# Forgetting attention and a SwiGLU block on one core: a planner with new transfer times, loads ahead of transposes, one load for both gate sums, one pool of four PSUM banks

## The chip, the core and the metric

The kernel runs on one core of a Trainium2 chip. The time is the device time of one execution in microseconds; less is better. The profile is taken from one execution of its own, whose time stands beside its span in the table below.

Engine names as in the profile: PE (matmuls; PEld is its weight load), DVE, ACT, POOL, and SP (SyncE, which only issues DMA transfers). Sixteen DMA engines carry all transfers.

## The reference, cut to what matters

Inputs are q, k, v with 8 batches, 8 heads, 576 positions and 64 values per head, and a forget gate f per batch, head and position. Attention is causal, with a decay from the running sum of log f:

```
scores = scale * q @ k.T
cum    = cumsum(log(clip(f, 1e-4, 1)))          # the "gate sum" of a head, 576 numbers
scores = where(causal, -1e9, scores + cum[:, None] - cum[None, :])
attn   = softmax(scores) @ v                     # 64 heads in all
x      = attn.transpose(0, 2, 1, 3).reshape(4608, 512)
out    = (silu(x @ w_gate) * (x @ w_val)) @ w_out    # 512 -> 1536 -> 512
```

The row term `cum[:, None]` drops out of the softmax, so the kernel only adds the column term.

## The kernel before

**Pairs and units.** The 64 heads are handled as 32 pairs (p = 0 to 31, four pairs per batch); the two heads of a pair lie in partitions 0 to 63 and 64 to 127. A pair has two units: g = 0 holds row blocks 0 to 3 of 64 queries, g = 1 row blocks 4 to 8. The first four pairs run all their g = 0 units first, then g = 1; later pairs run g = 1, then g = 0.

**What a pair goes through.** K and Q are loaded as float32 (`load_pair`, L325: 96 and 72 partitions), cast to bf16 on POOL (L350, L352), transposed on PE into a PSUM bank (L364) and copied to `kt` and `qz` (L378, L380). The gate sums of all heads are computed once at the start and stored to DRAM (`cum_f`, L312); for each later pair they are loaded again, each head's row repeated over 64 partitions, into a tile `cb` of 128 partitions by 576 numbers. That is one transfer per head (L332):

```
for h in range(2):
    loads["cb", p, h] = pl.op({"SP": 600}, lambda e, h=h: nc.sync.dma_start(
        out=pl.buf(("cb", p))[64 * h:64 * h + 64, :],
        in_=cum_dram[2 * p + h:2 * p + h + 1, :].to_broadcast((64, S))), ...
```

Scores come from PE (L399, with the causal mask added by L403), DVE adds the gate sum and takes the minimum (L415), ACT takes the exponential with its row sum (L429), POOL multiplies by the reciprocal sum into `pk` (L464). P is then transposed: for pairs 0 to 7 on PE (L488, L493), for pairs 8 to 31 by a DMA transpose on SP's queue (L476), 19 slices of 128 by 128 for g = 1 and 6 for g = 0. PE forms the weighted sum with V (L514), and DVE or ACT copies it into `xT` (L538), a ring of 2560 token columns.

**Feed-forward.** Tokens go through in tiles of 256 or 512: gate and value products (L595), tanh on ACT (L601), two DVE products (L603, L606), projection in rows of 128 tokens (`project`, L620), a copy to `ot` (L630, L632) and a store (L637).

**The order.** Nothing is scheduled at run time. `Plan.order` lists all operations once, when the program is built: each operation has one or more possible engines with a planned duration, a priority, and a planned time from its end to its users; transfers have a planned time on the wire (`dma`). Repeatedly the operation that can start earliest is taken, lower priority number first. Buffers are given out pool by pool in a fixed turn. Each engine then runs its operations strictly in that order and waits where data or a buffer is not there. SP's queue, too, is one fixed sequence of loads, transposes and stores. `after` lists make the planner place an operation later; they are no waits on the chip. `SPARE` makes the planner prefer POOL over ACT or DVE for some operations. Attention has lower priority numbers than feed-forward, so it goes first where both could start.

**PSUM.** Eight banks: `sp` 2 (scores), `tx` 2 (K and Q transposes, weighted sums), `gv` 3 (gate and value products, P transposes on PE, the last projections), `op` 1 (projection).

**Buffers of the loads.** `kf`, `qf` 2 each, `kt`, `qz` and `cb` 5 each, `pk` and `pT` 2 each per unit kind, `vf` 2, `ot` 2.

Of the kernel before, what the change touches and what calls it, by code (L numbers as in the profile page):

```python
# [15 lines left out]
HUGE = 3.0e38  # L16


class Op:
    __slots__ = ("n", "engs", "fn", "reads", "writes", "prio", "lat", "dma", "deps", "start", "end", "eng", "after", "holds", "bias")  # L20

    def __init__(self, n, engs, fn, reads, writes, prio, lat, dma, after, holds):
        self.holds = list(holds)
        self.n, self.engs, self.fn, self.reads, self.writes = n, engs, fn, reads, writes
        self.prio, self.lat, self.dma, self.after = prio, lat, dma, after
        self.start = self.end = self.eng = None
        self.bias = {}


class Plan:  # L30
# [6 lines left out]
    def __init__(self):  # L37
        self.ops, self.pools, self.home, self.where, self.turn = [], {}, {}, {}, {}
# [4 lines left out]
    def key(self, key, pool, turn=None):  # L43
        self.home[key], self.turn[key] = pool, turn
# [9 lines left out]
    def order(self):  # L54
# [14 lines left out]
        turn = {name: [] for name in self.pools}  # L69
# [4 lines left out]
        for k in sorted(self.home, key=rank):  # L74
            turn[self.home[k]].append(k)
        taken = {name: 0 for name in self.pools}
# [3 lines left out]
        free = {e: 0 for e in ("PE", "DVE", "ACT", "POOL", "SP")}  # L80
        wire = {True: 0, False: 0}
        ready = {o.n: 0 for o in self.ops if not waiting[o.n]}
        done = []

        def room(o):

            at, take = 0, []
            for k in o.writes:
                if k not in self.home or k in self.where:
                    continue  # L90
                name, best = self.home[k], None
                if turn[name][taken[name] + sum(name == self.home[x] for x, _ in take)] != k:
# [10 lines left out]
                take.append((k, best[1]))  # L103
            return at, take

        while ready:
            best = None
            for n, r in ready.items():
                o = self.ops[n]
                got = room(o)  # L110
                if got is None:
                    continue
                for e, dur in o.engs.items():
                    s = max(r, got[0], free[e])
                    c = (s + o.bias.get(e, 0), o.prio, n, e, dur, got[1])
                    if best is None or c[:4] < best[:4]:
                        best = c
# [4 lines left out]
            s -= o.bias.get(e, 0)  # L122
            for k, b in take:
                name = self.home[k]
                self.where[k] = b
                slots[name][b] = k
                taken[name] += 1
            o.start, o.eng = s, e
            free[e] = s + dur
            if o.dma:  # L130
                q = e == "POOL"
                at = max(wire[q], free[e] + 600)
# [3 lines left out]
                o.end = wire[q] + 1200  # L136
# [21 lines left out]
def kernel(  # L158
# [41 lines left out]
    AHEAD = 8  # L200
    BEHIND = 5
    BOTH = 8
    LAG = 3.5
    EASE = (2.5, 3)
    SPARE = {"ACT": 300, "DVE": 600}
    EARLY = {0: 4.3, 1: 7.8}
    FREE = 8
    STARTUP = "p0 f9 f0 p1 c1 p2 c2 p3 v00 c3 v01 wg0 wv0 wg2 wv2 v02 v03 v04 wg4 wv4 wg8 wv8 p4 c4 wo0 p5 c5 wo4 wo8 p6 c6 v10 v11 v12"
# [48 lines left out]
    bufs("gv", [P, 512], F32, 3, ps)  # L257
    bufs("op", [P, 512], F32, 1, ps)
# [36 lines left out]
    def gates(key, parts, np_, prio):  # L295
        x = lambda: pl.buf(key)[0:np_, :]
        for n, (a, z, src) in enumerate(parts):
            loads["f", key, n] = pl.op({"SP": 600}, lambda e, a=a, z=z, src=src: nc.sync.dma_start(out=pl.buf(key)[a:z, :], in_=src),
                                       (), [(key, 0)] + [key] * (n == 0), prio + n * .01, dma=500)
# [8 lines left out]
    for p in range(NDIRECT):  # L308
# [4 lines left out]
          [("fa", 3)], ["cum_dram"], -120, dma=500, lat=0, holds=["fa"])  # L313
# [6 lines left out]
    def load_pair(p):  # L320
        b, hp = divmod(p, NPB)
        s = first[p]
        for name, src, pr in (("k", k, 0), ("q", q, .1)):
# [4 lines left out]
                (), [(name + "f", p)], (-99 + 3 * p if p < NPB else s) + pr, dma=1130 if name == "k" else 980, after=[sums[p - 3, 0 if p - 3 >= NPB else 1]] if p >= NPB else [])  # L328
        if p >= NDIRECT:
            pl.key(("cb", p), "cb")  # L330
            for h in range(2):
                loads["cb", p, h] = pl.op({"SP": 600}, lambda e, h=h: nc.sync.dma_start(  # L332
                    out=pl.buf(("cb", p))[64 * h:64 * h + 64, :],
                    in_=cum_dram[2 * p + h:2 * p + h + 1, :].to_broadcast((64, S))),
                    ["cum_dram"], [("cb", p), (("cb", p), 3)], -98.5 + 3 * p if p < NPB else s + .2, dma=560)

    def prepare(p):
        s = first[p]
        for name in ("k", "q"):
# [19 lines left out]
            pl.key(tk, "tx")  # L359
# [5 lines left out]
            pl.op({"PE": KC * (KR / 2.4 + 2.5)}, transpose, [bk], [tk], s - 1, lat=200)  # L365
            halves = [(0, P, None)] if name == "k" else [(0, 64, 0), (64, 128, 1)]
            ok = ("kt", p) if name == "k" else ("qz", p)
            pl.key(ok, ok[0])
            for a, z, h in halves:
# [11 lines left out]
                pl.op({"ACT": 600, "DVE": 680}, evac, [tk] + ([("z", "qz", p)] if h is not None and p < 5 else []), [ok], s - .9)  # L381
# [4 lines left out]
    def scores(p, g):  # L386
# [3 lines left out]
        for n, bank in enumerate(BANKS[g]):  # L390
# [14 lines left out]
            pl.op({"PE": mm(*cols)}, mult, [("kt", p), ("qz", p), "mask"], [sk], pr, lat=220)  # L405
# [29 lines left out]
    def normalize(p, g):  # L435
# [11 lines left out]
        pl.op({"DVE": 95}, lambda e: nc.vector.reciprocal(lr(), lr()), [("lr", p, g)], [("l2", p, g)], s, lat=100, holds=[("lr", p, g)])  # L447
# [27 lines left out]
        if (p, g) not in ON_PE:  # L475
            pl.op({"SP": 550 + 150 * NSL[g]}, lambda e: nc.sync.dma_start_transpose(  # L476
                out=pl.buf(tk), in_=pl.buf(kk).rearrange("p s k -> p (s k)")),
                [kk], [tk], s - 1, dma=186 * NSL[g])
            return
        for a in range(0, NSL[g], 8):  # L480
            z = min(a + 8, NSL[g])
            bk = ("tt", p, g, a)
            pl.key(bk, "gv")
# [5 lines left out]
            pl.op({"PE": 56 * (z - a)}, transpose, [kk], [bk], s, lat=200)  # L489
# [6 lines left out]
    def weighted(p, gs):  # L496
        b, hp = divmod(p, NPB)
        keys, cost = [], 190
        for g in gs:
            pl.key(("xo", p, g), "tx", at[p, gs[0]] + (LAG if p >= NPB else EASE[g]))  # L500
# [15 lines left out]
        pl.op({"PE": cost}, mult, [("pT", p, g) for g in gs] + [("vt", b, c) for c in range(max(HI[g] for g in gs) // 2 + 1)],  # L516
              keys, at[p, gs[0]], lat=220, holds=[("vt", b)])
        for g in gs:
            spread(p, g)

    def spread(p, g):
# [5 lines left out]
        for a, z in ((0, cut), (cut, w)):  # L527
# [12 lines left out]
            o = pl.op({"ACT": QB * (z - a) * .833 + 130, "DVE": QB * (z - a) / .96 + 85}, evac, [xk],  # L540
                      [("x", hp, n) for n in range(tok[0] // QB, tok[1] // QB)], s)
            evacs.append((o, tok))

    def load_v(b):
        for c in range(5):
# [4 lines left out]
            if b:  # L550
                s = at[b * NPB, 1] + c * .1 - .5
# [3 lines left out]
                (), [fk], s, dma=1500 * n / P, after=wait)  # L555
# [7 lines left out]
    def weights():  # L563
# [4 lines left out]
        for a, z in zip(cuts, cuts[1:]):  # L568
            for nm, wt, src in (("wg", wg, moe_w_gate), ("wv", wv, moe_w_val)):
                piece({"POOL": 600}, lambda e, wt=wt, src=src, a=a, z=z: nc.gpsimd.dma_start(  # L570
                    out=wt[:, :, a:z], in_=src[:, a:z].rearrange("(ko p) n -> p ko n", p=P)),
                    (), [(nm, n) for n in range(a // P, z // P)], 2 + a / 256, dma=4.7 * (z - a) + 900)
        for c in range(0, KF, 4):
            piece({"POOL": 600}, lambda e, c=c: nc.gpsimd.dma_start(
                out=wo[:, c:c + 4, :], in_=moe_w_out[c * P:(c + 4) * P, :].rearrange("(ko p) n -> p ko n", p=P)),
                (), [("wo", n) for n in range(c, c + 4)], 7 + c / 4, dma=3300)
# [3 lines left out]
    def gate(t, tok, n):  # L580
# [3 lines left out]
        for u in range(KF // nf):  # L584
# [3 lines left out]
            for nm, wt in (("wg", wg), ("wv", wv)):  # L588
                bk = (nm, t, u)
                pl.key(bk, "gv", EARLY[t] + u * .55 if t in EARLY else None)  # L590
# [18 lines left out]
    def project(t, tok, n):  # L609
        nf = 512 // n  # L610
        for ms in range(n // P):
            bk = ("op", t, ms)
            end = (t, ms) == (len(TILES) - 1, n // P - 1)
            pl.key(bk, "gv" if t >= len(TILES) - 2 and (ms or t == len(TILES) - 1) else "op")
            pr = 1000 + (t + 1) * 20 + (ms + .5) * 12 * P / n
            for f0 in range(0, KF, 4):
                def mult(e, f0=f0, ms=ms, bk=bk):
                    for fc in range(f0, f0 + 4):
                        hh = pl.buf(("hh", t, fc // nf))
                        nc.tensor.matmul(pl.buf(bk), hh[:, (fc % nf) * n + ms * P:(fc % nf) * n + ms * P + P], wo[:, fc, :],  # L620
                                         start=fc == 0, stop=fc == KF - 1)
                pl.op({"PE": mm(*[DM] * 4)}, mult, [("hh", t, fc // nf) for fc in range(f0, f0 + 4)] +
                      [("wo", fc) for fc in range(f0, f0 + 4)] + ([(bk, f0)] if f0 else []), [bk, (bk, f0 + 4)], pr, lat=220)
            ok = ("ot", t, ms)
            pl.key(ok, "ot")

            for a, z in ((0, DM // 2), (DM // 2, DM)) if end else ((0, DM),):
                def evac(e, bk=bk, ok=ok, a=a, z=z):
                    if e == "ACT":
                        nc.scalar.mul(pl.buf(ok)[:, a:z], pl.buf(bk)[:, a:z], 0.5)  # L630
                    else:
                        nc.vector.tensor_scalar(pl.buf(ok)[:, a:z], pl.buf(bk)[:, a:z], 0.5, None, op0=ALU.mult)  # L632
                engs = {"ACT": 495, "DVE": 620}
                if end:
                    engs = {"ACT": 290} if a else {"DVE": 340}
                pl.op(engs, evac, [bk], [ok, (ok, a)], pr - 5000)
                pl.op({"SP": 560}, lambda e, ms=ms, ok=ok, a=a, z=z: nc.sync.dma_start(  # L637
                    out=out[tok + ms * P:tok + ms * P + P, a:z], in_=pl.buf(ok)[:, a:z]),
                    [(ok, a)], [("out", t, ms, a)], pr - 5000, dma=680 * (z - a) // DM, lat=0, holds=[ok])
# [14 lines left out]
    for x in STARTUP.split():  # L654
# [7 lines left out]
        elif x[0] == "c":  # L662
            line += [loads["cb", n, h] for h in range(2)]
# [55 lines left out]
```

## Time and profile before

| | |
|---|---|
| median of 3 runs | 438.39 us (437.34 to 438.73) |
| profiled execution, its time | 437.73 us |
| its span, first to last instruction | 436.0 us |
| granted TensorE clock | 1.00 |
| busy share PE, DVE, ACT, POOL | 92%, 80%, 69%, 58% |
| HBM read, written | 47.33 MB, 9.58 MB |
| DMA packets | 143956 |
| first and last DMA transpose of P issued | 108.6 and 350.4 us |
| last weighted sum on PE | 357.1 us |

Busy times are unions over the span. Matmuls overlap, so that a busy PE is not PE at its peak. A wait is put down to what came last before it ended. A line such as L476 is the line of the kernel that issued the instruction. In the DMA view, packets are what the DMA engines recorded, "under 512 B" counts the small ones among them, and a share is the time that packets took, over 16 engines' time in the window.

### The profile page before, as it was taken

To read this page: it belongs to the slowest core of one execution; us is meant where nothing else is said; L and a number is where in the kernel's file an instruction comes from. 1 tells how busy PE (TensorE), PEld (TensorE's weight loads), DVE (VectorE), ACT (ScalarE), POOL (GpSimd) and SP (SyncE) were. 2 spreads that over 40 slices of the span, in tenths; PEclk is the share of its full clock that TensorE was granted. 3 is DMA by queue.
4 is the path that set the end of the run, shared out by engine and by line. 5 is a ranking of instruction groups with operands and counts; after the bars stand their busy time and mean duration, and the time that the engine had idled before them with its cause. 6 is when DMAs were issued, how large, how long until landed. Compare 5 with 4: busy or idle time off the path is not lost.

```text
span 436.0 us, 9859 instructions
## 1 busy us (share of the span) xinstructions
PE 402.5 (92%) x3192; PEld 229.2 (53%) x3192; DVE 347.9 (80%) x1081; ACT 302.8 (69%) x848; POOL 252.1 (58%) x452
## 2 busy tenths in 40 slices
PE   2578999998999998989999999999999999999996
PEld 1436777755454454444555554555445444457662
DVE  6788799798999798977999998999989665365340
ACT  6799789989877968776798777677678633232321
POOL 5699748748956855886668768938875600000000
PEclk9999999999999999999999999999999999999999
DMA  7999999637978998999999999999994640010112
GB/s 195 212 188 227 203 207 215 165 101 212 192 169 187 225 215 188 194 218 234 198 207 213 222 219 206 189 223 207 202 199 100 117 108 26 24 50 24 50 50 72
DMA packets 143956, 72.51 MB, mean 166 GB/s; under 512 B 118560, under 2 KB 130592, under 8 KB 143904
## 3 DMA queue, kind: packets, MB, share of 16 engines
q1 hardware_dynamic: 137732, 66.57, 71.9%
q0 software_dynamic: 5808, 4.72, 7.1%
q10 hardware_dynamic: 364, 0.59, 0.6%
q8 instruction: 25, 0.41, 0.4%
q14 instruction: 27, 0.22, 0.2%
HBM read 47.33 MB, written 9.58 MB: 131 GB/s over the span
## 4 chain that ended last, share of the span: by engine, by line
PE 60%; DVE 12%; DMA 10%; ACT 9%; POOL 4%; issue 4%; SPq 1%; DVEq 0%; ACTq 0%; POOLq 0%
PE gv L595 29%; PE op L620 15%; DMA qf<-in_q_dram 7%; PE sp L399 5%; DVE t L415 4%; PE tx L514 4%; ACT eo L429 3%; ACT e L429 2%; PE tx L364 2%; DVE qz L380 2%; DVE th L603 2%; POOL pk L464 2%; DMA pT<-pk 2%; PE gv L620 2%; DVE hh L606 2%
## 5 line engine op out<-in xcount | busy, mean ns | idle before, releaser
L415 DVE CUSTOM_DVE_ANT_0 t<-sp,cb 128x512 f32<-128x512 f32 (+7 forms) x288 | 130.4, 476 | 12.2 <-PE sp L403 5.9
L464 POOL TENSOR_SCALAR pk<-e,lr 128x512 bf16<-128x512 f32 (+3 forms) x186 | 97.7, 529 | 33.3 <-DVE tm L415 17.6
L595 PE MATMUL gv<-xT,wv 128*128 128x512 bf16 (+1 forms) x528 | 111.2, 340 | 0.2 <-DVE th L603 0.2
L595 PE MATMUL gv<-xT,wg 128*128 128x512 bf16 (+1 forms) x528 | 111.2, 340 | 0.2
L601 ACT ACTIVATE th<-gv 128x512 f32<-128x512 f32 x108 | 64.1, 594 | 61.0 <-PE gv L595 59.7
L603 DVE SCALAR_TENSOR_TENSOR th<-th,gv 128x512 f32<-128x512 f32 x108 | 73.9, 684 | 37.5 <-ACT th L601 37.1
L429 ACT ACTIVATE e<-t,tm 128x448 f32<-128x448 f32 (+4 forms) x160 | 88.8, 556 | 20.2 <-DVE tm L415 19.6
L620 PE MATMUL op<-wo,hh 128*128 128x512 bf16 x396 | 100.7, 379 | 2.1 <-DVE ot L632 1.3
L606 DVE TENSOR_TENSOR hh<-th,gv 128x512 bf16<-128x512 f32 x108 | 73.4, 685 | 10.3 <-PE op L620 4.1
L399 PE MATMUL sp<-kt,qz 128*128 128x448 bf16 (+4 forms) x320 | 72.3, 294 | 9.2 <-DVE tm L415 8.1
L429 ACT ACTIVATE eo<-t,tm 128x256 f32<-128x256 f32 (+3 forms) x128 | 71.2, 556 | 6.4 <-DVE tm L415 6.0
L595 PEld LDWEIGHTS <-wg 128*128 128x128 bf16 x528 | 48.9, 98 | 37.1 <-issue 0.2
L464 POOL TENSOR_SCALAR pk<-eo,lr 128x128 bf16<-128x128 f32 (+3 forms) x123 | 65.3, 531 | 2.5 <-ACT th L601 1.0
L595 PEld LDWEIGHTS <-wv 128*128 128x128 bf16 x528 | 47.8, 98 | 34.9 <-issue 0.3
L620 PEld LDWEIGHTS <-hh 128*128 128x128 bf16 x432 | 39.6, 98 | 41.8 <-issue 2.3
L403 PE MATMUL sp<-mask,ident 128*128 128x64 bf16 x288 | 48.1, 197 | 0.0
L399 PEld LDWEIGHTS <-qz 128*128 128x128 bf16 x320 | 30.6, 100 | 24.5 <-DVE qz L380 2.7
L350 POOL TENSOR_SCALAR qb<-qf 72x1024 bf16<-72x1024 f32 x31 | 32.9, 1062 | 14.8 <-DMA qf<-in_q_dram 7.2
L352 POOL CAST kb<-kf 96x768 bf16<-96x768 f32 x31 | 25.4, 820 | 27.4 <-DMA kf<-in_k_dram 19.3
L403 PEld LDWEIGHTS <-ident 128*128 128x128 bf16 x288 | 27.0, 100 | 21.3 <-issue 11.0
L557 POOL CAST vt<-vf 128x512 bf16<-128x512 f32 (+1 forms) x40 | 24.3, 608 | 17.4 <-DMA vf<-in_v_dram 17.2
L514 PE MATMUL tx<-pT,vt 128*64 128x320 bf16 (+4 forms) x448 | 29.7, 266 | 1.5 <-ACT e L429 0.5
(61 smaller groups left out, 393.2 us busy)
## 6 DMA issues: line engine op xcount, KB each, us to landing
out_dram<-ot SPq DMA_DIRECT2D x35, 256.0 KB, 2.4
kf<-in_k_dram SPq DMA_DIRECT2D x31, 288.0 KB, 6.3
qf<-in_q_dram SPq DMA_DIRECT2D x31, 288.0 KB
cb<-cum_f SPq DMA_DIRECT2D x62, 144.0 KB, 4.7
vf<-in_v_dram SPq DMA_DIRECT2D x32, 256.0 KB, 4.4
wo<-in_moe_w_out_dram POOLq DMA_DIRECT2D x3, 512.0 KB, 9.9
vf<-in_v_dram SPq DMA_DIRECT2D x8, 128.0 KB
wg<-in_moe_w_gate_dram POOLq DMA_DIRECT2D x2, 512.0 KB, 9.1
```

The costliest lines, as they stand in the source:

```text
L350: eng[e].tensor_scalar(dst, src, -scale, 1.0, op0=ALU.mult, op1=ALU.mult)
L399: nc.tensor.matmul(sp[:, o:o + z - a], qz[:, i, :, :].rearrange("p h r -> p (h r)"), kt[:, a:z], start=True, stop=not last)
L403: nc.tensor.matmul(sp[:, o - QB:o], ident, mask, start=False, stop=True)
L415: nc.vector.tensor_tensor_reduce(out=pl.buf(tk)[:, a:z], in0=pl.buf(sk)[:, o:o + z - a], in1=pl.buf(("cb", p))[:, a:z], scale=1.0, scalar= ...
L429: nc.scalar.activation(pl.buf(ek)[:, :L], pl.buf(tk)[:, :L], AF.Exp, bias=pl.buf(("tm", p, g))[:, i:i + 1], scale=-1.0, accum_out=pl.buf(( ...
L464: eng[e].tensor_scalar(dst, src, r, 1.0, op0=ALU.mult, op1=ALU.mult)
L514: nc.tensor.matmul(xo[r, 0:QB * n], vt[:, c, 2 * hp + h, :], pT[:, a:a + n, 64 * h:64 * h + 64], start=(c == 0), stop=(c == nch - 1))
L595: nc.tensor.matmul(pl.buf(bk)[:, j * n:j * n + n], wt[:, ko, fc * P:fc * P + P], xT[:, ko, x0:x0 + n], start=ko == 0, stop=ko == KD - 1)
L601: pl.op({"ACT": 487}, lambda e, u=u: nc.scalar.activation(pl.buf(("th", t, u)), pl.buf(("wg", t, u)), AF.Tanh, scale=0.5), [("wg", t, u)], ...
L603: pl.op({"DVE": 605}, lambda e, u=u: nc.vector.scalar_tensor_tensor(pl.buf(("th", t, u)), pl.buf(("th", t, u)), 1.0, pl.buf(("wg", t, u)), ...
L606: pl.op({"DVE": 605}, lambda e, u=u: nc.vector.tensor_mul(pl.buf(("hh", t, u)), pl.buf(("th", t, u)), pl.buf(("wv", t, u))), [("u", t, u), ...
L620: nc.tensor.matmul(pl.buf(bk), hh[:, (fc % nf) * n + ms * P:(fc % nf) * n + ms * P + P], wo[:, fc, :], start=fc == 0, stop=fc == KF - 1)
```

## The change

The change has these parts:

- One load per pair brings both gate sums: the source pattern names 2 rows, 64 repeats with step 0, and 576 numbers; the destination is the whole tile of 128 partitions. (The DRAM tensor and its bytes are the same.)
- Loads of K, Q, gate sums and V get a priority 8 units earlier (`SOON`), so that they come ahead of P's transposes (`s - 1`). K and Q of pair p may be planned once the last exponential of pair p - 4 is (`BACK`, 3 before), the gate sums once that of p - 5 is (`CBACK`, no such bound before).
- `gv` has four banks, `op` none. Each pool can now have lines with their own turn: in `gv` "f" (gate and value products, at most 3 banks), "p" (P's transposes, at most 2) and "o" (projection, at most 2); in `tx` "q" (K and Q) and "v" (weighted sums). The hand-set turns `LAG`, `EASE` and `EARLY` go. A line that is later in rank lets an earlier one go first where that could start within 800 ns (`SLACK`).
- The planner's numbers: transfers by new times, a start of each transfer 2.0 us (2.55 us on POOL's queue) after its issue, SP held by a DMA transpose, PE operations before 25 us planned at double length (`COLD`), and two engines that read one PSUM bank kept apart.
- K and Q's transposes claim their target `kt` or `qz` already when PE transposes them.
- ACT may take normalization for pairs 0 to 3 (`FREE`; pairs 0 to 7 before); `SPARE` is larger; the list of loads at the start is longer and slightly reordered.
- The last projection is done in two halves of 256 columns, each with a bank of its own.
- The reuse of `xT` columns waits, in the planner, before the weighted sum instead of before its copy.

```diff
-            for h in range(2):
-                loads["cb", p, h] = pl.op({"SP": 600}, lambda e, h=h: nc.sync.dma_start(
-                    out=pl.buf(("cb", p))[64 * h:64 * h + 64, :],
-                    in_=cum_dram[2 * p + h:2 * p + h + 1, :].to_broadcast((64, S))),
-                    ["cum_dram"], [("cb", p), (("cb", p), 3)], -98.5 + 3 * p if p < NPB else s + .2, dma=560)
+            loads["cb", p] = pl.op({"SP": 600}, lambda e: nc.sync.dma_start(
+                out=pl.buf(("cb", p)), in_=bass.AP(cum_dram.tensor, cum_dram.offset + 2 * p * S, [[S, 2], [0, 64], [1, S]])),
+                ["cum_dram"], [("cb", p), (("cb", p), 3)], -98.5 + 3 * p if p < NPB else s - SOON + .2, dma=1140, after=[sums[p - CBACK, 0 if p - CBACK >= NPB else 1]] if p >= NPB + 1 else [])
...
-                (), [(name + "f", p)], (-99 + 3 * p if p < NPB else s) + pr, dma=1130 if name == "k" else 980, after=[sums[p - 3, 0 if p - 3 >= NPB else 1]] if p >= NPB else [])
+                (), [(name + "f", p)], (-99 + 3 * p if p < NPB else s - SOON) + pr, dma=1060, after=[sums[p - BACK, 0 if p - BACK >= NPB else 1]] if p >= NPB else [])
...
-    AHEAD = 8
+    MOST = (("p", 2), ("o", 2), ("f", 3))
+    AHEAD = 6
...
-    SPARE = {"ACT": 300, "DVE": 600}
-    FREE = 8
+    SPARE = {"ACT": 500, "DVE": 900}
+    FREE = 4
+    SLACK = 800
+    SOON = 8
+    BACK = 4
+    CBACK = 5
...
-    bufs("gv", [P, 512], F32, 3, ps)
-    bufs("op", [P, 512], F32, 1, ps)
+    bufs("gv", [P, 512], F32, 4, ps)
+    pl.banks = {"sp", "tx", "gv"}
+    pl.most = {("gv", x): n for x, n in MOST}
...
+            if e == "PE" and s < COLD:
+                dur *= 2
...
             if o.dma:
                 q = e == "POOL"
-                at = max(wire[q], free[e] + 600)
+                at = max(wire[q], s + (2550 if q else 2000))
...
-                o.end = wire[q] + 1200
+                if o.ring:
+                    free[e] = max(free[e], wire[q] - 1450)
+                o.end = wire[q] + 1100
...
-            pl.op({"SP": 550 + 150 * NSL[g]}, lambda e: nc.sync.dma_start_transpose(
+            pl.op({"SP": 300 + 153 * NSL[g]}, lambda e: nc.sync.dma_start_transpose(
                 out=pl.buf(tk), in_=pl.buf(kk).rearrange("p s k -> p (s k)")),
-                [kk], [tk], s - 1, dma=186 * NSL[g])
+                [kk], [tk], s - 1, dma=500 + 118 * NSL[g]).ring = True
...
             for a, z in ((0, DM // 2), (DM // 2, DM)) if end else ((0, DM),):
+                bk = ("op", t, ms, a)
+                pl.key(bk, "gv", line="o")
+                for f0 in range(0, KF, 4):
+                    def mult(e, f0=f0, ms=ms, bk=bk, a=a, z=z):
+                        for fc in range(f0, f0 + 4):
+                            hh = pl.buf(("hh", t, fc // nf))
+                            nc.tensor.matmul(pl.buf(bk)[:, 0:z - a], hh[:, (fc % nf) * n + ms * P:(fc % nf) * n + ms * P + P], wo[:, fc, a:z],
+                                             start=fc == 0, stop=fc == KF - 1)
```

More of the change, by code (lines that the diff above doesn't have):

```diff
@@ L16 @@
 HUGE = 3.0e38
+COLD = 25000
 class Op:
-    __slots__ = ("n", "engs", "fn", "reads", "writes", "prio", "lat", "dma", "deps", "start", "end", "eng", "after", "holds", "bias")
+    __slots__ = ("n", "engs", "fn", "reads", "writes", "prio", "lat", "dma", "deps", "start", "end", "eng", "after", "holds", "bias", "ring")
     def __init__(self, n, engs, fn, reads, writes, prio, lat, dma, after, holds):
@@ L27, in __init__, with key @@
         self.bias = {}
+        self.ring = False
 class Plan:
     def __init__(self):
-        self.ops, self.pools, self.home, self.where, self.turn = [], {}, {}, {}, {}
+        self.slack = 0
+        self.ops, self.pools, self.home, self.where, self.turn, self.banks = [], {}, {}, {}, {}, set()
+        self.line, self.most = {}, {}
     def pool(self, name, bufs):
         self.pools[name] = bufs
-    def key(self, key, pool, turn=None):
-        self.home[key], self.turn[key] = pool, turn
+    def key(self, key, pool, turn=None, line=None):
+        self.home[key], self.turn[key], self.line[key] = pool, turn, line
     def buf(self, key):
@@ L68, in order @@
                 kids.setdefault(d.n, []).append(o)
-        turn = {name: [] for name in self.pools}
+        turn = {}
         def rank(k):
@@ L79, in order, with room @@
         slots = {name: [None] * len(b) for name, b in self.pools.items()}
-        free = {e: 0 for e in ("PE", "DVE", "ACT", "POOL", "SP")}
+        free = {e: 700 for e in ("PE", "DVE", "ACT", "POOL", "SP")}
         wire = {True: 0, False: 0}
         ready = {o.n: 0 for o in self.ops if not waiting[o.n]}
-        done = []
-        def room(o):
+        done, using = [], {}
+        def room(o, now=None):
             at, take = 0, []
@@ L91, in room @@
                 name, best = self.home[k], None
-                if turn[name][taken[name] + sum(name == self.home[x] for x, _ in take)] != k:
-                    return None
+                x = name, self.line[k]
+                mine = sum(x == (self.home[y], self.line[y]) for y, _ in take)
+                if turn[x][taken[x] + mine] != k:
+                    return None
+                if x in self.most:
+                    held = sum(y is not None and left[y] > 0 and self.line[y] == x[1] for y in slots[name])
+                    if held + mine >= self.most[x]:
+                        return None
                 for n, held in enumerate(slots[name]):
@@ L103, in room @@
                 take.append((k, best[1]))
+            if now is not None:
+                for k, _ in take:
+                    for x in lines[self.home[k]]:
+                        if x[1] != self.line[k] and taken[x] < len(turn[x]):
+                            y = turn[x][taken[x]]
+                            q = opener[y]
+                            if rank(y) < rank(k) and q.n in ready and ready[q.n] <= max(now, at) + self.slack and room(q) is not None:
+                                return None
             return at, take
@@ L114, in order @@
                     s = max(r, got[0], free[e])
+                    for k in o.reads:
+                        if k in using and using[k][0] != e:
+                            s = max(s, using[k][1])
                     c = (s + o.bias.get(e, 0), o.prio, n, e, dur, got[1])
@@ L358, in prepare @@
             tk = ("tt", name, p)
-            pl.key(tk, "tx")
+            pl.key(tk, "tx", line="q")
+            ok = ("kt", p) if name == "k" else ("qz", p)
+            pl.key(ok, ok[0])
             def transpose(e, bk=bk, tk=tk, KR=KR, KC=KC):
@@ L380, in evac @@
                         nc.vector.tensor_copy(dst, src)
-                pl.op({"ACT": 600, "DVE": 680}, evac, [tk] + ([("z", "qz", p)] if h is not None and p < 5 else []), [ok], s - .9)
+                pl.op({"ACT": 600, "DVE": 680}, evac, [tk] + ([("z", "qz", p)] if h is not None and p < 5 else []), [ok, (ok, "done")], s - .9)
     def epool(i):
@@ L499, in weighted @@
         for g in gs:
[L500 removed]
+            pl.key(("xo", p, g), "tx", line="v")
             w = HI[g] - LO[g] + 1
@@ L515, in mult, with spread @@
                                          start=(c == 0), stop=(c == nch - 1))
-        pl.op({"PE": cost}, mult, [("pT", p, g) for g in gs] + [("vt", b, c) for c in range(max(HI[g] for g in gs) // 2 + 1)],
+        o = pl.op({"PE": cost}, mult, [("pT", p, g) for g in gs] + [("vt", b, c) for c in range(max(HI[g] for g in gs) // 2 + 1)],
               keys, at[p, gs[0]], lat=220, holds=[("vt", b)])
         for g in gs:
-            spread(p, g)
-    def spread(p, g):
+            spread(p, g, o)
+    def spread(p, g, mult):
         b, hp = divmod(p, NPB)
@@ L571, in weights @@
                     out=wt[:, :, a:z], in_=src[:, a:z].rearrange("(ko p) n -> p ko n", p=P)),
-                    (), [(nm, n) for n in range(a // P, z // P)], 2 + a / 256, dma=4.7 * (z - a) + 900)
+                    (), [(nm, n) for n in range(a // P, z // P)], 2 + a / 256, dma=5.1 * (z - a) + 880)
         for c in range(0, KF, 4):
@@ L575, in weights @@
                 out=wo[:, c:c + 4, :], in_=moe_w_out[c * P:(c + 4) * P, :].rearrange("(ko p) n -> p ko n", p=P)),
-                (), [("wo", n) for n in range(c, c + 4)], 7 + c / 4, dma=3300)
+                (), [("wo", n) for n in range(c, c + 4)], 7 + c / 4, dma=3500)
     gates_of = {}
@@ L611, in project @@
         for ms in range(n // P):
[L612 to L623, printed above, removed]
@@ L624, in project @@
             ok = ("ot", t, ms)
             pl.key(ok, "ot")
+            pr = 1000 + (t + 1) * 20 + (ms + .5) * 12 * P / n
+            end = (t, ms) == (len(TILES) - 1, n // P - 1)
             for a, z in ((0, DM // 2), (DM // 2, DM)) if end else ((0, DM),):
+                bk = ("op", t, ms, a)
[6 more added lines that the diff above has]
+                                             start=fc == 0, stop=fc == KF - 1)
+                    pl.op({"PE": mm(*[z - a] * 4)}, mult, [("hh", t, fc // nf) for fc in range(f0, f0 + 4)] +
+                          [("wo", fc) for fc in range(f0, f0 + 4)] + ([(bk, f0)] if f0 else []), [bk, (bk, f0 + 4)], pr, lat=220)
@@ L628, in evac @@
                 def evac(e, bk=bk, ok=ok, a=a, z=z):
                     if e == "ACT":
-                        nc.scalar.mul(pl.buf(ok)[:, a:z], pl.buf(bk)[:, a:z], 0.5)
+                        nc.scalar.mul(pl.buf(ok)[:, a:z], pl.buf(bk)[:, 0:z - a], 0.5)
                     else:
[L632 to L635, printed above, removed]
@@ L636, in project @@
-                pl.op(engs, evac, [bk], [ok, (ok, a)], pr - 5000)
+                        nc.vector.tensor_scalar(pl.buf(ok)[:, a:z], pl.buf(bk)[:, 0:z - a], 0.5, None, op0=ALU.mult)
+                pl.op({"ACT": (z - a) * .833 + 70, "DVE": (z - a) / .96 + 85}, evac, [bk], [ok, (ok, a)], pr - 5000)
                 pl.op({"SP": 560}, lambda e, ms=ms, ok=ok, a=a, z=z: nc.sync.dma_start(
                     out=out[tok + ms * P:tok + ms * P + P, a:z], in_=pl.buf(ok)[:, a:z]),
-                    [(ok, a)], [("out", t, ms, a)], pr - 5000, dma=680 * (z - a) // DM, lat=0, holds=[ok])
+                    [(ok, a)], [("out", t, ms, a)], pr - 5000, dma=950 * (z - a) // DM, lat=0, holds=[ok])
@@ L662 @@
         elif x[0] == "c":
-            line += [loads["cb", n, h] for h in range(2)]
+            line.append(loads["cb", n])
         elif x[0] == "v":
```

47 lines of the change are left out of this document (25 added, 22 removed).

## The prediction

> **What bounds the kernel now.** I read the profile page first, then the busy times by stretch, the waits, SyncE's issues in time order, and last the DMA view of three short stretches. The stretches are the first pairs (0 to 108 us, P transposed on PE), the steady part (108 to 347 us, P transposed by DMA) and the tail of pure feed-forward:
>
> ```profile
> 0.00:108.00 108.00, 85.59 (x899) 61.47 (x900) 89.20 (x300) 92.92 (x249) 78.74 (x150) 1.00 0.92 194
> 108.00:347.00 239.00, 232.09 (x1788) 120.04 (x1787) 218.03 (x721) 184.07 (x556) 172.05 (x301) 1.00 0.99 197
> 347.00:436.00 89.00, 84.83 (x508) 47.65 (x505) 40.65 (x61) 25.77 (x44) 1.34 (x4) 1.00 0.16 51
> ```
>
> Columns: window, length, busy us of PE, PEld, DVE, ACT, POOL, granted clock, DMA share, GB/s. PE is busy 232.1 of 239 us in the steady part, so PE sets the pace, at full clock. But the DMA share stands at 0.99 beside it: a second resource is nearly full and idle only in the tail. The other half of the picture is SyncE, which issues loads and transposes in one fixed order:
>
> ```profile
> SPq L476 <- POOL pk L464: 63.3, 21, 7.1
> ...
> POOL kb L352 <- DMA kf<-in_k_dram: 19.3, 10, 6.6
> ...
> PE tx L364 <- POOL qb L350: 4.7, 6, 1.5
> ```
>
> ```profile
> 264.63 0.87 SPq L325 DMA_DIRECT2D kf<-in_k_dram  x1
> 265.56 0.41 SPq L325 DMA_DIRECT2D qf<-in_q_dram  x1
> 266.08 5.87 SPq L476 DMA_TRANSPOSE pT<-pk  x1
> ```
>
> SyncE stands 63 us in front of transposes whose P isn't ready, loads behind them come late, POOL waits for K (19.3 us) and PE a little for POOL. A transpose then holds SyncE for 5.87 us. The order of loads therefore has something to give, but PE has only 239 - 232.1 = 6.9 us idle in this part.
>
> How full is a DMA engine? The page's queue rows and the DMA view of three stretches (121.0 to 123.0: two gate-sum halves; 338.9 to 341.3: transposes alone; 366 to 369: one output store):
>
> ```profile
> q1 hardware_dynamic: 137732, 66.57, 71.9%
> q10 hardware_dynamic: 364, 0.59, 0.6%
> cb<-cum_f SPq DMA_DIRECT2D x62, 144.0 KB, 4.7
> ```
>
> ```profile
> DMA packets 160, 0.30 MB, mean 148 GB/s; under 512 B 32, under 2 KB 32, under 8 KB 160
> q1 hardware_dynamic: 160, 0.30, 41.9%
> ```
>
> ```profile
> DMA packets 1957, 0.50 MB, mean 209 GB/s; under 512 B 1957, under 2 KB 1957, under 8 KB 1957
> ```
>
> ```profile
> DMA packets 144, 0.26 MB, mean 87 GB/s; under 512 B 16, under 2 KB 16, under 8 KB 144
> q1 hardware_dynamic: 144, 0.26, 23.3%
> ```
>
> A store of 128 rows leaves 128 data packets and 16 small ones; the two gate-sum halves (64 rows of 2304 B each) leave 128 and 32. So each transfer leaves one small packet per DMA engine that carried it, 16 of 16. q10 carried only the first pair's K (96 rows x 2 heads = 192 packets) and Q (72 x 2 = 144): 336, and 28 are left, 16 for K and 12 for Q. 72 rows do not divide by 16, and 12 is the largest number up to 16 that divides them. [...]
>
> **The change part by part.**
>
> *One load for both gate sums.* 62 issues become 31; SyncE saves 31 x 0.59 us, hidden, as SyncE waits anyway. The bytes stay. But the merged source is written as 2 rows x 64 repeats x 576 numbers: its outermost dimension is 2, where each half had 64. No transfer of before has an outermost 2, so the cost is bounded from both sides: on 16 engines 8 packets each, as now; on 2 engines 64 packets each. I take 2, by the Q row, the only one whose count 16 does not divide. A 2304 B packet: 0.419 x 16 x 2.0 us / 128 = 105 ns in the second fence, at most, as packets overlap; from the store, 0.233 x 16 x 3 us / 128 = 87 ns for 2048 B, or 98 ns by size. I take 98: 64 x 98 ns = 6.3 us on each of two engines, where eight packets took 0.8.
>
> [...]
>
> What else do these two engines carry per pair? Transposes: 25 slices x 128 rows / 16 = 200 packets of 256 B at 19.6 ns (2.4 us x 16 / 1957) = 3.9 us. V: 72 packets of 256 B, 1.4. K: 12 of 1536 B at 65 ns, 0.8; Q: 12 of 2048 B at 87 ns, 1.0; output: 9 such, 0.8. With the halves' 0.8 that is 8.7 us in a pair's period of 239 / 23 = 10.4 us. Merged, it is 8.7 - 0.8 + 6.3 = 14.2 us: these two engines no longer fit into PE's period. [...] Cover there is, but of the wrong kind: gate sums are issued some 40 us ahead of their first use (262.3 us against 302.8 for pair 28), and that hides a late transfer, not a rate. PE's order is fixed, so feed-forward work of the tail can't move into the holes.
>
> The end, by these engines' whole work until the last transpose: gate sums 31 x 6.3 = 195, transposes 24 x 3.9 = 94, V 32 x 1.4 = 45, K and Q 32 x 1.8 = 58, weights 7.1% of 436 = 31 (queue q0), outputs before the tail 22 x 8 x 87 ns = 15, gates 2: 440 us. Idle at the start (first packet at 2.7 us, the cumulative sums in DRAM only at about 12.8): 8. From the last transpose's issue (ends 351.7) to the span's end: 84, and 437.7 - 436.0 = 1.7 outside the span. Together 534. With each packet at its quickest in the trace (93 ns for 2304 B, 18 ns for 256 B) the 440 are about 415, and the end is 509. By period: 437.7 + 23 x 3.8 = 525, plus what the start loses (0 to 20 us; three gate sums one behind the other now take 19 us, before units that followed within some 5 us). I take 525.
>
> *Loads go ahead of transposes* (priority 8 units earlier, K and Q held to 4 pairs, gate sums to 5; buffers as before). At best PE's 6.9 us in the steady part go, most of it waits like the 4.7 above; at worst loads take the engines when a transpose is due and the weighted sum comes late by a pair's K and Q (1.8 us) now and then: -5 to +5 alone. When two engines are behind, an earlier issue only lengthens their queue: 0.
>
> *Four PSUM banks in one pool* for gate products, projection and P's transposes (at most 3, 2, 2), and the weighted sums' bank no longer timed by hand. PE's idle time before projection and gate products is 2.1 + 0.2 us: a gain of at most 2, a loss of the same size if a projection sits on a bank that a gate product wants.
>
> *ACT may normalize in pairs 0 to 3 instead of 0 to 7.* POOL did 309 of 320 of these, so at most 11 x 0.53 us moves to POOL, which is idle 18 us between 50 and 100 us: 0.
>
> *The last projection in two halves with a bank each.* 12 more matmuls, of half the width: no more columns; 12 more weight loads at 98 ns lie beside streams of about 107. ACT's last copy waited for DVE's on the same bank (431.93 + 0.42, then 432.38): now it needn't: -0.5.
>
> *Costs in the planner and the rest* (transfer times, cold PE until 25 us, K/Q transposes claiming their target): order only. Together these parts are -3, from -8 to +6, as long as the DMA engines keep up; they are within the rounding of the 525. The median of the runs, 438.39, stands 0.7 above the profiled 437.73; no correction.
>
> **Rivals.**
> 1. *The merged load runs on 16 engines.* For: both halves did, and nothing on the SBUF side (128 rows) hinders. Against: the 12 engines of Q. Then only the order changes: 438.4 - 3 - 0.5 = about 434 (430 to 442). This is the case on the other side; it decides if more than about 8 engines carry the load, since with 16 packets each (8.7 - 0.8 + 1.6 = 9.5 us) the period of 10.4 still holds them.
> 2. *Two engines, but hidden.* The 40 us of lead cover it. For it the two engines would need 6.3 us free per pair; they have 10.4 - 7.9 = 2.5. Only if packets of two transfers overlap far better than the shares of 1.0 show does it hold: about 440.
> 3. *Two engines, and SyncE starves them:* each transpose holds SyncE until its slowest engine is nearly through, and two idle microseconds per pair come on top: 24 x 2 = 48 us, about 570. The upper end.
>
> **Numbers.** Two engines set the pace: 0.84 (rival 3's share of that 0.1), with a range of its own from 490 to 570; 16 engines: 0.10; hidden: 0.06. The range of 475 to 575 leaves out the two fast cases and little of the slow one. A measurement of this kernel tells about 0.3%, 1.3 us, from no change. Faster: 0.07 of the 16-engine case and 0.01 of the hidden one; same 0.03; slower 0.89.
>
> **What would show it.** Small packets: 62 x 16 = 992 become 31 x 2 = 62, so q1 falls from 137732 to about 136802; on 16 engines it would be 137236. The mean DMA share falls to about 0.8 in the steady part while loads land far later than 6 us, transposes hold SyncE for 8 us and more, and PE waits for POOL's casts and for pT, some 3 to 4 us per pair, spread over all 24. The tail stays at 80 to 85 us. Wrong it would be if q1 shows 137236, if PE's busy share in the steady part stays above 0.95, or if the lost time sits in the start alone.

## The result and the profile after

The changed kernel takes 534.37 us (median of 4 runs, 532.2 to 535.47) against 437.87 us (4 runs): 1.2205 times the time, 95% interval 1.2145 to 1.2266. The profiled execution took 533.52 us with a span of 531.7.

Busy times by stretch of the changed kernel (columns as before; the second stretch ends with the last DMA transpose of P):

```profile
0.00:108.00 108.00, 67.47 (x654) 50.64 (x655) 67.65 (x228) 67.68 (x178) 64.21 (x127) 0.91 0.70 144
108.00:450.00 342.00, 282.30 (x2076) 144.07 (x2074) 241.23 (x795) 210.57 (x625) 189.43 (x334) 0.93 1.03 156
450.00:531.70 81.70, 78.09 (x479) 45.70 (x476) 37.83 (x56) 23.50 (x40) 0.00 (x0) 0.99 0.14 45
```

PE is no longer the pace: 282 of 342 us in the second stretch, 67 of 108 at the start. The tail behind the last DMA transpose is 81.5 us long (85.6 before). In the second stretch 156 GB/s moved (197 in the steady part before), yet the DMA share did not fall; the last section says why. The queue rows of the page and the gate sums' issues show what became of the loads:

```profile
q1 hardware_dynamic: 136802, 66.57, 75.7%
q10 hardware_dynamic: 364, 0.59, 0.5%
cb<-cum_f SPq DMA_DIRECT2D x31, 288.0 KB
```

136802 packets is the number that 2 small packets per merged load give; 16 would have given 137236. The DMA view of 5 us inside one such load (281.4 to 286.4 us) shows the two engines at work:

```profile
DMA packets 112, 0.25 MB, mean 51 GB/s; under 512 B 2, under 2 KB 2, under 8 KB 112
q1 hardware_dynamic: 112, 0.25, 13.0%
```

13.0% of sixteen engines is 2.1 engines, 0.13 x 16 x 5 us / 110 = 95 ns per 2304 B packet, and nothing else moves. SyncE in time order shows who stands behind the load (start, length):

```profile
276.04 0.37 SPq L362 DMA_DIRECT2D qf<-in_q_dram  x1
276.69 0.39 SPq L588 DMA_DIRECT2D vf<-in_v_dram  x1
277.13 0.53 SPq L368 DMA_DIRECT2D cb<-cum_f  x1
277.76 9.29 SPq L511 DMA_TRANSPOSE pT<-pk  x1
287.15 1.67 SPq L588 DMA_DIRECT2D vf<-in_v_dram  x2
```

The transpose holds SyncE from 277.76 us for 9.29 us, where the one shown of before held it for 5.87. For five of these microseconds (281.4 to 286.4 above) nothing but gate sums moves. The wait then reaches PE through K and Q:

```profile
POOL qb L385 <- DMA qf<-in_q_dram: 35.4, 9, 12.9
POOL pk L499 <- DMA pT<-pk: 34.7, 10, 9.1
...
PE tx L401 <- POOL kb L387: 28.7, 11, 6.0
```

### The profile page after: what moved, and what is told of

It is laid out like the page before. It is cut to its first block, busy times and chain, and to the rows that moved or that the text cites. A ratio compares the mean times of both kernels' runs of the same rounds, so it can differ in the third digit from the quotient of the medians.

```text
span 531.7 us, 9842 instructions
## 1 busy us (share of the span) xinstructions
PE 427.9 (80%) x3204; PEld 240.4 (45%) x3204; DVE 346.7 (65%) x1078; ACT 301.8 (57%) x843; POOL 253.6 (48%) x460
## 3 DMA queue, kind: packets, MB, share of 16 engines
q1 hardware_dynamic: 136802, 66.57, 75.7%
## 4 chain that ended last, share of the span: by engine, by line
PE 41%; DMA 37%; POOL 8%; issue 5%; DVE 4%; SPq 3%; ACT 1%; POOLq 0%; DVEq 0%; ACTq 0%
PE gv L630 22%; PE gv L658 11%; DMA vf<-in_v_dram 9%; DMA cb<-cum_f 8%; DMA kf<-in_k_dram 6%; DMA qf<-in_q_dram 6%; DMA pT<-pk 6%; POOL pk L499 5%; PE sp L434 3%; PE tx L549 2%; DVE t L450 2%; SPq L511 2%; PE tx L401 2%; DMA cb<-in_f_dram 1%; POOL qb L385 1%
## 5 line engine op out<-in xcount | busy, mean ns | idle before, releaser
L499 POOL TENSOR_SCALAR pk<-e,lr 128x256 bf16<-128x256 f32 (+3 forms) x191 | 100.7, 531 | 65.5 <-DMA pT<-pk 34.7
L630 PE MATMUL gv<-xT,wv 128*128 128x512 bf16 (+1 forms) x528 | 116.8, 354 | 2.7 <-DMA wv<-in_moe_w_val_dram 2.7
L630 PE MATMUL gv<-xT,wg 128*128 128x512 bf16 (+1 forms) x528 | 117.1, 354 | 2.0 <-DMA wg<-in_moe_w_gate_dram 1.9
L658 PE MATMUL gv<-wo,hh 128*128 128x512 bf16 (+1 forms) x444 | 113.2, 392 | 0.0
L434 PE MATMUL sp<-kt,qz 128*128 128x448 bf16 (+4 forms) x320 | 75.7, 302 | 20.7 <-DVE tm L450 19.8
L499 POOL TENSOR_SCALAR pk<-eo,lr 128x384 bf16<-128x384 f32 (+2 forms) x127 | 67.8, 534 | 16.4 <-DVE tm L450 15.2
L658 PEld LDWEIGHTS <-hh 128*128 128x128 bf16 x444 | 41.9, 102 | 43.1 <-issue 8.2
L401 PE MATMUL tx<-ident,kb 96*128 96x96 bf16 x192 | 15.7, 226 | 34.0 <-POOL kb L387 28.7
L415 DVE COPY qz<-tx 64x576 bf16<-64x576 bf16 x32 | 24.1, 753 | 24.4 <-PE tx L401 22.2
L665 ACT ACTIVATE ot<-gv 128x512 f32<-128x512 f32 (+1 forms) x23 | 13.4, 584 | 46.7 <-PE gv L658 46.7
```

Of the source, the lines that this page charges most:

```text
L401: nc.tensor.transpose(half(tk)[:, KR * j:KR * j + KR], src[0:KR, j, :], ident[0:KR, 0:KR])
L434: nc.tensor.matmul(sp[:, o:o + z - a], qz[:, i, :, :].rearrange("p h r -> p (h r)"), kt[:, a:z], start=True, stop=not last)
L499: eng[e].tensor_scalar(dst, src, r, 1.0, op0=ALU.mult, op1=ALU.mult)
L630: nc.tensor.matmul(pl.buf(bk)[:, j * n:j * n + n], wt[:, ko, fc * P:fc * P + P], xT[:, ko, x0:x0 + n], start=ko == 0, stop=ko == KD - 1)
L658: nc.tensor.matmul(pl.buf(bk)[:, 0:z - a], hh[:, (fc % nf) * n + ms * P:(fc % nf) * n + ms * P + P], wo[:, fc, a:z], start=fc == 0, stop=f ...
```

## The experiments

All ratios are to the kernel before, measured beside it. "Halves" means that a pair's gate sums come in two loads of 64 partitions, as before.

**e1: the new order with halves.** In short, `lambda e: [nc.sync.dma_start(out=cb[64*h:64*h+64], in_=cum_dram[2*p+h].to_broadcast((64, S))) for h in range(2)]` in place of the merged load, at the same place of the order.

> The changed kernel with its order untouched; only each merged gate-sum load is issued as two loads of 64 partitions again. Two engines too few for their share (theory): the whole loss goes, 434 us (430 to 442), q1 back to 137732 packets, PE busy about 0.97 of the steady part. The new order is what costs (rival): stays near 530 us.

Measured 423.86 us, ratio 0.9687 (0.9639 to 0.9736), q1 137732. The whole loss is the merged load's, 110 us, and the rest of the change makes the kernel faster by 13.5 us, more than the 4 that I had given it; the time lies below the expected 430 to 442. Its stretches:

```profile
0.00:108.00 108.00, 87.53 (x938) 63.31 (x939) 92.56 (x322) 92.40 (x252) 87.25 (x168) 1.00 0.99 207
108.00:347.00 239.00, 238.98 (x1835) 123.91 (x1834) 216.90 (x709) 184.46 (x556) 165.43 (x293) 1.00 0.98 196
```

PE is busy 238.98 of 239 us: all 6.9 us of idle time that it had in this part are gone.

**e2: the old order with the merged load.** In the kernel before, the first of the two operations issues the merged load, the second nothing.

> The kernel before, order and PSUM banks untouched; only the two gate-sum loads of a pair become the merged one at the place of the first. Theory (two engines' share): 520 to 540 us, pair period 14 to 14.5 us, q1 136802 packets. Rival (the new order costs): 438 us.

557.81 us, ratio 1.2755 (1.2685 to 1.2824), q1 136802. The merged load alone does it, and in the old order it costs more (120 us), above the range that I gave. The period came as expected: 14.5 us, over the 16 pairs from the transpose at 165.5 to that at 396.7 us. What the range left out is the start: the first transpose is issued at 158.1 us, 49.5 us later than before. The new order is no cause of the loss; with it the loss is smaller.

**e3, e5, e6: how many engines.** Each head's gate sums are stored R times in DRAM, one copy behind the other, so that the same single load has an outermost dimension of 2R (the line of the load; the store of the copies is left out here):

```diff
-in_=bass.AP(cum_dram.tensor, cum_dram.offset + 2 * p * S, [[S, 2], [0, 64], [1, S]])
+in_=bass.AP(cum_dram.tensor, cum_dram.offset + 2 * p * R * S, [[S, 2 * R], [0, 64 // R], [1, S]])
```

> The changed kernel with each head's gate sums stored twice in DRAM, so that the merged load's outermost dimension is 4 instead of 2. Theory (a rate): 32 packets, 3.1 us on each of four engines, 11.0 us of work against a period of 10.4: 0.6 x 23 = 14 us over the halves, about 450 us (440 to 460). Rival (a wait of the load's length in front of each transpose, whatever the period): (3.1 - 0.8) / (6.3 - 0.8) of the loss, about 475 us. Packets of q1: 136802 + 62 = 136864, and 64 more packets of the stored copies.

> The changed kernel with four stored copies, so that the merged load's outermost dimension is 8. Theory (a rate): 16 packets, 1.6 us on each of eight engines, 8.7 - 0.8 + 1.6 = 9.5 us a pair against the 10.2 that the halves in this order run at: no loss but for the start (copies of 1.5 us in front of the first loads), 426 us (423 to 431). Rival (a wait of the load's length before each transpose): (1.6 - 0.8) / (6.3 - 0.8) of the 110 us, 440 us.

> The changed kernel with eight stored copies, the outermost dimension 16: one load again, on all engines. 8 packets on each, as with two halves, and 31 issues fewer on SyncE, which waits anyway; eight copies stored once cost some 3 us at the start. 426 us (422 to 430). If one issue fewer were worth something by itself: under 422.

| outermost | us | ratio, interval |
|---|---|---|
| 2 (the change) | 534.37 | 1.2205, 1.2145 to 1.2266 |
| 4 (e3) | 456.27 | 1.0427, 1.0362 to 1.0492 |
| 8 (e5) | 428.43 | 0.9751, 0.9711 to 0.9792 |
| 16 (e6) | 428.16 | 0.9757, 0.9714 to 0.9801 |
| halves (e1) | 423.86 | 0.9687, 0.9639 to 0.9736 |

The page's queue rows of e3, e5 and e6:

```profile
q1 hardware_dynamic: 136928, 66.71, 79.2%
q1 hardware_dynamic: 137180, 67.01, 76.1%
q1 hardware_dynamic: 137684, 67.60, 72.9%
```

Over the change's 136802 these are 62, 186 and 434 more small packets (2, 6 and 14 more for each of 31 loads) and 64, 192 and 448 packets of the stored copies. With 2 small packets the window above showed 2.1 busy engines; at one packet an engine these loads ran on 4, 8 and 16. For them the packet count alone says so.

Eight engines cost no more than sixteen (428.43 and 428.16 us), though a load has 16 packets on each instead of 8, an estimated 1.6 us instead of 0.8; a cost by the load's length would have put 16 us between them. So here it is a rate: it hurt where the engines' estimated work per pair passes the period (11.0 us on four engines against 10.4), and not where it stays below (9.5 on eight against 10.2). One load on 16 engines is not better than two: it is 0.7 percentage points slower, with intervals that overlap. The transposes of e5 and e6 (number, min/median/max of SyncE's hold in ns, start of the first and of the last) show where this lies:

```profile
L515 SPq DMA_TRANSPOSE pT<-pk x48: 1210/2540/6243, 106.7 to 345.0; - x48
L515 SPq DMA_TRANSPOSE pT<-pk x48: 1210/2526/5252, 106.4 to 344.2; - x48
```

From the first to the last they take 238.3 and 237.8 us, as with halves (237.8 in e1, below). The difference lies ahead of the first transpose, 4 us later than e1's, where the copies are stored; that the copies cost it was not tried.

**e4 and e12: where the loss sits.** e4 merges for odd pairs only; e12 for pairs from 10 on (`if p >= 10 else` halves).

> The changed kernel with the merged load for odd pairs alone, two halves for even pairs. Theory (a rate with some pairs of lead): mean work of the two engines (8.7 + 14.2) / 2 = 11.5 us a pair against 10.4, so about 25 us over the halves, near 460 us. Rival (each merged load is waited for in full): half the loss, near 482 us.

> The changed kernel with two halves for pairs 1 to 9 and the merged load from pair 10 on. If the loss has two places (46 us before the first DMA transpose of P, 64 us after it by the period of 13.0 against 10.2 us), this keeps the second: first transpose at 102 to 108 us, 480 to 495 us. If each merged load costs the same wherever it stands: 22 of 31 of the 110, 502 us.

e4: 472.31 us (four runs from 466.75 to 475.92; ratio 1.0734, 1.062 to 1.0849), between both. e12: 495.72 us (1.1277, 1.1209 to 1.1344), just past the range for "two places". The transposes tell it better. The change, e1, e4, e12 and e3:

```profile
L511 SPq DMA_TRANSPOSE pT<-pk x48: 1209/2427/9990, 147.9 to 450.2; - x48
```

```profile
L512 SPq DMA_TRANSPOSE pT<-pk x48: 1211/2464/5186, 102.2 to 340.0; - x48
```

```profile
L513 SPq DMA_TRANSPOSE pT<-pk x48: 1212/2536/9609, 121.0 to 388.0; - x48
```

```profile
L513 SPq DMA_TRANSPOSE pT<-pk x48: 1209/2460/10378, 107.0 to 412.1; - x48
```

```profile
L515 SPq DMA_TRANSPOSE pT<-pk x48: 1209/2543/7351, 116.7 to 370.9; - x48
```

From first to last transpose e1 needs 237.8 us, the change 302.3 (64.5 more), e4 267.0 (29 more; the rate said 25), e12 305.1 (67 more), e3 254.2 (16 more; the rate said 14). Ahead of the first transpose the change loses 45.7 us, e4 18.8, e3 14.5, and e12, where nine of the thirteen pairs loaded there come in halves, 4.8. So there are two places, the rate holds in the steady one, and in e3 and e4 I had left out the start.

**e7 to e11: what the 13.5 us of the rest come from.** Each takes one part back from e1, and e10 puts one part into the kernel before. The edits in short:

```
 e7   SOON = 0, BACK = 3, no CBACK, V at -0.5
 e8   transfer times, start, hold of SP, cold PE: as before
 e9   bufs("gv", ..., 3), bufs("op", ..., 1); projections in op, but for most of the last two tiles
 e10  before: loads at s - 8, K and Q after pair p - 4, gate sums after p - 5
 e11  SOON = 0 alone
```

> The changed kernel with two halves per pair, but loads at the priority and with the bounds of before (no 8 units earlier, K and Q to 3 pairs, no bound for gate sums, V as before); everything else of the change stays. Theory (the order's gain of 13.5 us comes from loads in front of transposes, as SyncE stood 63 us before them and POOL waited for K): most of the gain goes, 432 to 437 us. Rival (it comes from the banks or from the planner's numbers): stays at 424 to 428.

> The changed kernel with two halves per pair, but the planner's transfer times, its start of a transfer, SyncE's hold by a transpose and the cold PE as before; loads ahead and banks as changed. Theory (loads ahead carry the gain): 424 to 428. Rival (the numbers carry it): 432 to 437.

> The changed kernel with two halves per pair and PSUM as before: three banks for gate products and P's transposes, one for the projection (the last two tiles' projections still in the three). If the pool of four carries part of the 13.5 us: 428 to 434. If it carries nothing: 422 to 426. The waits of before (2.3 us before projection and gate products) speak for the second.

> The kernel before with one part of the change: loads of K, Q, V and gate sums 8 units earlier in priority, with the bounds of 4 and 5 pairs; numbers, banks and two halves as before. Theory (loads ahead carry most of the gain by themselves): 426 to 432. Rival (they do so only with the other parts): 436 to 445.

> The changed kernel with two halves per pair, and only the 8 units of priority taken back; the bounds of 4 and 5 pairs stay. This tells what lost 45 us when both were taken back: if the missing bound for gate sums let them stand on SyncE in front of everything, waiting for a free buffer, this is 424 to 436 us; if it was the priority, it is near 468.

| | us | ratio, interval |
|---|---|---|
| e7 loads not ahead, bounds off | 468.58 | 1.0669, 1.0634 to 1.0704 |
| e8 old numbers | 428.73 | 0.977, 0.9722 to 0.9818 |
| e9 old banks | 432.29 | 0.9844, 0.979 to 0.9898 |
| e10 before, loads ahead | 438.06 | 0.9969, 0.994 to 0.9998 |
| e11 priority back | 435.08 | 0.9899, 0.9842 to 0.9956 |

e7 was a miss: 45 us lost, not 10. One of its SyncE waits is 1.0 us in e1 and 4.0 in e11:

```profile
SPq L368 <- DVE tm L451: 54.3, 12, 13.5
```

SyncE stands 54 us in front of gate-sum loads that want a `cb` buffer still in use, and everything behind them stands too. e11 keeps the bounds and lands at 435. From e11 to e7 two bounds go (K and Q's, gate sums'), and V's priority differs a little as well. That the gate sums' bound is the cause is likely by this row, but not isolated.

Against e1's 0.9687 the numbers are worth 0.8 points (e8's interval overlaps e1's, and its time lies just above the 424 to 428 expected), the banks 1.6 and the priority 2.1. Together that is more than the 3.1 of all, and loads ahead alone give the kernel before 0.3 (e10). My theory that loads ahead carry most of the gain by themselves is wrong: the parts seem to need one another. No run takes back the other parts (`SPARE`, `FREE`, `SLACK`, the list at the start, the halves of the last projection). Every run here is one order out of the planner, and a changed number moves many operations, so differences of a few tenths of a point between orders should not be read as the price of a part.

## Why the prediction was right, point by point

- *Two engines:* right, by the packet count (136802) and the 2.1 busy engines. Loads with an outermost dimension of 2, 4, 8 and 16 left 2, 4, 8 and 16 small packets. Joining two halves into one transfer of 128 partitions cost 110 us here, where the joined pattern begins with 2. That other transfers wait for these two engines was measured in one stretch: from 281.4 to 286.4 us nothing but gate sums moved, at 51 GB/s. Why they wait is not shown.
- *98 ns a packet:* 95. That packets overlap shows in the stretch of transposes alone before the change (338.9 to 341.3 us: `q1 hardware_dynamic: 1957, 0.50, 112.3%`). The 93 and 18 ns called the quickest in the trace are not quite that; some packets of these sizes took 91 and 15.
- *The sum by the engines' whole work:* 440 + 8 for the last transpose's end, measured 451.4; 84 for the rest, measured 531.7 - 451.4 = 80.3; in all 534 against 533.5. With packet times that leave 415 to 440, so close a fit is partly luck. The forecast of 525 was drawn below this sum by the other route.
- *The sum by period* erred twice, with opposite signs. The period: 14.2 us while loads still come (measured 14.5 from the transpose at 236.0 to that at 424.2 us, 13 pairs), but the first five pairs after the start still live on gate sums fetched ahead (11.6 us a pair up to 205.8), and the last three have no gate sums left to load (5 to 11 us): 302.3 - 241.8 = 60.5 us more, where 23 x 3.8 = 87 was put down. The start: 147.9 - 108.6 = 39 us, where 0 to 20 was put down. That the two errors, with a tail 4 us shorter, leave 525 only 9 us off is luck. The mis-sized term is the lead: 13 merged loads are issued ahead of the first transpose, 5.5 us longer each on two engines, 71 us in all, of which 39 show. Here the lead moved the cost forward; it did not spread it.
- *"Together these parts are -3, from -8 to +6":* mis-sized as well, at -13.5 us in e1, outside its range. The idle 6.9 us of the steady part went in full, as the best case said, but they were no bound for the whole: of the 14.4 us by which e1's span is shorter, 6.4 lie ahead of the first transpose (102.2 against 108.6 us), 4.0 between first and last, and 4.0 behind the last (81.6 against 85.6 us). The start I had not looked at, and the banks, put at 2 us at most from PE's waits of 2.3, are worth 1.6 points (7 us) in e9. A wait list prices the waits of the order that ran; it does not price the orders that a bank makes possible.
- *Rival 1* had its time too high (434, 430 to 442; halves give 424), its deciding point of about 8 engines right (e5 against e6). *Rival 3's* 2 us of starving per pair did not come: 14.5 against 14.2. Of a transpose's hold of SyncE the trace shows the end: three large ones late in the steady part of before let go at 330.1, 340.7 and 349.7 us, 1.3 to 1.4 us before their last packet ended (331.5, 342.1 and 351.0).
- *DMA share to fall to 0.8:* wrong, 1.03. See the last section.
- *SyncE held 8 us and more, a tail of 80 to 85:* a median hold of 8.8 us for the 24 large transposes (4.4 before), and 81.5 us. Right.
- *PE waits 3 to 4 us per pair for POOL's casts and pT, over all 24:* half right. From the first to the last transpose PE waited 43.3 us for the casts and 4.8 for pT, 2.0 a pair, and in the last 26 us not at all. PE's own busy time makes up 19 of the 60.5 us: 1815 matmuls took 254.1 us there at a clock of 0.93, where 1812 took 234.9 before at 1.00. The prediction had no term for the clock.

## What to carry to other kernels

Before merging two transfers, look at the outermost dimension of the merged pattern and count the small packets of the queue row: here a load that begins with 2 left 2 of them beside 2.1 busy engines, one that begins with 16 left 16. Then add up one engine's work over a period (here an estimated 14.2 us against 10.4), not the mean of sixteen; a transfer that is issued 40 us early is still paid for in that sum. And when a change mixes a good part with a bad one, put the bad one back alone: e1 beats the kernel before by 3.1%.

## What the runs showed that I had not expected

**Waiting packets count as busy.** In the changed kernel at 281 us, 20 packets of 256 B, the size of a transpose's, lasted 5.5 to 5.8 us each instead of 18 ns. They began before 281.3 us and ended at 286.8, just after the last gate sums at 286.4. The stretch from 277 to 291 us:

```profile
GB/s 302 338 249 257 243 293 246 246 156 169 234 214 51 53 53 46 53 53 53 53 53 46 53 53 46 53 45 64 288 293 289 289 243 193 248 255 147 223 203 198
q1 hardware_dynamic: 6130, 2.30, 126.1%
```

Two engines' rate of about 53 GB/s stands in the middle for more than 5 us, and the share is 126%. (The 13.0% of the window above leaves these packets out, as they began before it.) So the other engines did not get on with the transpose while the two late ones moved gate sums; why they wait is not shown, and the trace doesn't name a packet's engine. In such a stretch the DMA share is no measure of free engines; GB/s tells more.

**PE's clock fell.** The page's PE rows of the changed kernel, and a stretch at the start (59.8 to 70.0 us):

```profile
PE   2419679994869599796886959978898699999997
...
PEclk9999777996989799898998988997999799999999
```

```profile
59.80:70.00 10.20, 7.47 (x47) 4.96 (x45) 2.04 (x5) 4.31 (x9) 4.66 (x8) 0.50 0.69 134
```

The granted clock was 0.50 for 3.4 to 10.2 us at a time, 0.932 in the mean; before and in e1 it was 1.00. PE had waited ahead of each of these times: of the 3.4 us before, as long as the shortest of them, it was busy for 0.1 to 1.5. PE's busy time rose from 402.5 to 427.9 us with nearly the same work (12 matmuls more). Whether the waits bring the clock down, and what the lower clock adds to the 534 us, was not tried; PE also stood idle at times in the stretch shown (7.47 of 10.20 us busy).
